# Query tiles moved by one block, narrow products paired across heads, and the largest tile's heads in two PSUM tiles

## The chip, the cores and the metric

The kernel runs on one core of a Trainium2 chip. Five engines work side by side, each through its own instructions in program order: PE (matrix products and transposes), DVE (vector work, reductions, copies), ACT (exponentials and copies), POOL (vector work, and it issues some DMAs) and SP (it issues DMAs). They wait for each other by semaphores. The metric is the device time of one execution in microseconds (us), the median of several runs.

## What is computed

Two stages. First attention over 8 batches and 8 heads, 576 positions of 64 features, float32; a position sees its own block of 64 and all blocks before it. Then a mixture of experts over the 4608 positions: a gate chooses one of 8 experts for each position, every expert keeps the 80 positions with the largest gate weights, and two products (512 to 1024 to 512) are made for these.

```python
def _attn_ref(q, k, v):
    scores = scale * np.matmul(q, k.transpose(0, 1, 3, 2))
    mask = (pos // 64)[:, None] >= (pos // 64)[None, :]
    scores = np.where(mask, scores, -1000000000.0)
    scores = scores - np.max(scores, axis=-1, keepdims=True)
    attn = np.exp(scores)
    attn = attn / (np.sum(attn, axis=-1, keepdims=True) + 1e-09)
    return np.matmul(attn, v)

def _moe_ref(x, w_gate, w1, w2, capacity):
    logits = x @ w_gate
    expert_idx = np.argmax(logits, axis=1)
    ...
    for e in range(E):
        ...                     # the 80 largest gate weights of expert e
        h = np.maximum(x[tok_idx] @ w1[e], 0.0)
        out[tok_idx] = gate_w[tok_idx, None] * (h @ w2[e])
```

## The kernel before

**Pairs and turns.** The unit of attention is a pair of heads (`Pair`); there are 32. The 64 features of head 0 lie on partitions 0 to 63, those of head 1 on 64 to 127, so products of both heads run side by side in two halves of PE. The main loop (`for i in range(-3, n + 2)`) makes one turn per pair. A turn carries out the table `TURN`, an order written out by hand: each entry has an offset, a step and arguments, and acts on pair `i` + offset. So a turn mixes steps of up to six pairs. The instructions of an engine are in the order in which the table's steps issue them.

**Tiles.** The 9 blocks of queries are cut into tiles. Tile u (0 to 3) holds blocks 2u and 2u+1, 128 queries, and sees keys 0 to 128(u+1); its first block may not see the last 64 of them, and a product of `mrow` and `mneg` (L481) adds a large negative number there. Tile "4" holds block 8 of both heads, 64 queries each on 128 partitions, and sees all 576 keys (L490).

**PSUM.** The scores use a ring of two tiles of two banks, `sc`: first the largest tile ("3", both heads, 512 columns each), then tiles 2 and 0 together ("20"), tile 1 ("1") and tile 4 ("4"). All else on PE (transposes, values, gate) uses a ring of four tiles of one bank, `pm`.

**Steps of a pair.** `load` issues q and k (SP, L426), `load_v` issues v (POOL, L434 and L436). `prep` transposes q (0, with a scaling on POOL, L459) and k (1) on DVE (L456). `scores` makes the products (L474) and the mask (L481). `max` reduces each row on DVE (L495, L499 for tile 4). `soft` takes the exponential on ACT, with the sums of the rows (L503; L508 for tile 4). `back` transposes the exponentials on PE (L539; L522 for a piece named 44): A is tile 3, B tiles 1 and 2, C the rest; 16 narrow transposes each into two `pm` tiles. `take` copies a `pm` tile to SBUF, on ACT (L579) or DVE (L581) by the table `TAKE`. `values` multiplies with v (L569): 0 for positions 0 to 511 and 1 for the last 64. `flip` turns the result on DVE (L290) and stores it.

**The gate of a batch.** When the four pairs of a batch are done, nine steps (reciprocals, store, logits of two halves, and so on to the table of weights) are put on a list, `todo`; the three entries `step` of a turn take one each. The gate's work thus lies in three of a batch's four turns.

**Behind attention** the candidates are selected (line 700 on), gate weights are picked with one-hot products on PE (L822) from columns that POOL builds (L748), and the experts' products run (L894, L907).

## Time and profile before

| | us |
|---|---|
| median of 3 runs | 433.95 |
| lowest, highest | 432.39, 435.62 |
| profiled execution, its own time | 433.55 |
| its span in the trace | 431.8 |

| engine | busy, us | share of the span |
|---|---|---|
| PE | 407.2 | 94% |
| DVE | 281.9 | 65% |
| ACT | 272.7 | 63% |
| POOL | 137.4 | 32% |

Shares over the whole span mix two stages: attention takes the first three quarters, the experts the rest, where DVE and ACT are nearly idle. A view of a stretch says more than the page's averages, and the timeline of one turn more than both. PE overlaps the end of a matrix product with the beginning of the next, so in its timeline the starts are to be read, not the ends.

### The profile page before, as it was taken

What the parts mean: (1) busy time and instruction counts of PE and PEld (TensorE: products, weight loads), DVE (VectorE), ACT (ScalarE), POOL (GpSimd) and SP (SyncE); (2) the same over time, 40 slices, a digit from 0 to 9 for tenths busy, and PEclk for the clock granted to TensorE, in tenths of its full rate; (3) what the DMA queues carried; (4) which work ended last, traced back from release to release, by engine and by line L of the source; (5) the groups of instructions that cost most, each with busy time, mean ns of one, the idle gap of its engine ahead of it and who ended that gap; (6) DMA issues with size and microseconds to landing.
All of it is one profiled execution on the core that took longest, in us unless ns stands there. A gap on an engine that the chain in (4) does not pass through costs nothing. (4 is left out here: it accounts for less than half of the span.)

```text
span 431.8 us, 15597 instructions
## 1 busy us (share of the span) xinstructions
PE 407.2 (94%) x6454; PEld 287.8 (67%) x6454; DVE 281.9 (65%) x566; ACT 272.7 (63%) x868; POOL 137.4 (32%) x236
## 2 busy tenths in 40 slices
PE   7899999999999999999999999999886799999982
PEld 3566666666666666666666666666654699999981
DVE  5778888888797888879778887986584122111111
ACT  2988888798888879888887988889531110111000
POOL 9523343233344323334432333540037300000011
PEclk9999999999999999999999999999998699999998
DMA  9999958995997899499688969899986999999821
GB/s 149 156 130 180 176 93 199 147 181 120 210 177 105 204 137 188 118 206 179 106 199 134 177 137 208 181 372 330 275 176 187 325 304 310 286 320 328 310 81 37
DMA packets 201276, 84.59 MB, mean 196 GB/s; under 512 B 167677, under 2 KB 183805, under 8 KB 201200
## 3 DMA queue, kind: packets, MB, share of 16 engines
q1 hardware_dynamic: 190112, 53.37, 63.4%
q0 software_dynamic: 9888, 29.87, 22.2%
q8 instruction: 53, 0.87, 0.9%
q10 hardware_dynamic: 1200, 0.30, 0.3%
q14 instruction: 23, 0.19, 0.2%
HBM read 63.38 MB, written 20.33 MB: 194 GB/s over the span
## 5 line engine op out<-in xcount | busy, mean ns | idle before, releaser
L503 ACT ACTIVATE P<-sc,negm 128x128 f32<-128x128 f32 (+3 forms) x256 | 133.3, 531 | 9.9 <-DVE negm L495 8.3
L495 DVE TENSOR_REDUCE negm<-sc 128x2 f32<-128x1024 f32 (+3 forms) x128 | 100.5, 811 | 38.7 <-PE sc L481 38.7
L474 PE MATMUL sc<-T,T 64*128 64x128 f32 (+3 forms) x512 | 92.8, 460 | 1.9 <-DVE T L452 1.2
L539 PEld LDWEIGHTS pm<-ident,P 64*128 64x128 f32 x1536 | 55.7, 139 | 32.6 <-ACT xT L579 11.0
L459 POOL TENSOR_SCALAR T<-T 128x576 f32<-128x576 f32 x31 | 20.5, 661 | 171.9 <-DVE T L456 162.6
L539 PE MATMUL pm<-ident,P 64*128 64x64 f32 x1536 | 67.7, 227 | 2.0 <-ACT P L508 0.4
L569 PE MATMUL pm<-PT,vn 128*64 128x128 f32 (+1 forms) x512 | 60.7, 379 | 0.0
L474 PEld LDWEIGHTS sc<-T,T 64*128 64x128 f32 x512 | 41.7, 187 | 22.2 <-issue 7.1
L503 ACT ACTIVATION_READ_ACCUMULATOR P<-sc,negm 128x1 f32 x256 | 52.8, 206 | 0.0
L434 POOL DMA_DIRECT2D vn<-in_v_dram x64 | 50.1, 785 | 1.4 <-issue 1.4
L569 PE MATMUL pm<-PF,vn 128*64 128x64 f32 (+1 forms) x768 | 48.2, 247 | 0.9 <-ACT PF L579 0.9
L569 PEld LDWEIGHTS pm<-PT,vn 128*64 128x64 f32 x512 | 33.5, 137 | 22.9 <-issue 22.9
L456 DVE STREAM_TRANSPOSE T<-ld 128x576 f32<-128x576 f32 x62 | 47.4, 764 | 0.0
L894 PE MATMUL ps<-xsT,w 128*64 128x80 f32 x1024 | 42.4, 241 | 5.1 <-issue 5.0
L579 ACT COPY PF<-pm 128x512 f32<-128x512 f32 x64 | 34.4, 589 | 15.7 <-PE pm L539 15.7
L894 PEld LDWEIGHTS ps<-xsT,w 128*64 128x64 f32 x1024 | 39.1, 142 | 7.6 <-issue 6.9
L581 DVE COPY PT<-pm 128x512 f32<-128x512 f32 x64 | 43.5, 680 | 0.3 <-ACT xT L579 0.3
L490 PE MATMUL sc<-T,T 64*64 64x288 f32 x256 | 38.0, 415 | 0.6 <-ACT P L503 0.6
L919 ACT ACTIVATE hT<-ps 128x320 f32<-128x320 f32 x16 | 7.0, 437 | 49.3 <-PE ps L894 49.3
L579 ACT COPY PT<-pm 128x512 f32<-128x512 f32 x64 | 37.8, 591 | 0.0
L508 ACT ACTIVATE P<-sc,negm 128x576 f32<-128x576 f32 x32 | 23.7, 741 | 21.3 <-DVE negm L499 21.3
L569 PEld LDWEIGHTS pm<-PF,vn 128*64 128x64 f32 x768 | 32.0, 137 | 7.4 <-ACT PF L579 1.1
(185 smaller groups left out, 468.0 us busy)
## 6 DMA issues: line engine op xcount, KB each, us to landing
w<-in_moe_w_dram SPq DMA_DIRECT2D x48, 512.0 KB, 5.0
out_dram<-zero POOLq DMA_DIRECT2D x18, 512.0 KB, 4.2
ld<-in_q_dram SPq DMA_DIRECT2D x124, 72.0 KB, 3.9
ld<-in_k_dram SPq DMA_DIRECT2D x124, 72.0 KB, 3.9
vn<-in_v_dram POOLq DMA_DIRECT2D x64, 128.0 KB, 4.3
w<-in_moe_w_dram POOLq DMA_DIRECT2D x4, 2048.0 KB, 14.3
xs<-Y SPq DMA_DIRECT2D x28, 288.0 KB, 4.9
xs<-Y SPq DMA_DIRECT2D x16, 72.0 KB, 10.1
```

The source lines that it names most:

```text
L434: nc.gpsimd.dma_start(self.vn[:, h], v[b, h0 + h, 0:512].rearrange("(j p) d -> p j d", p=P))
L456: nc.vector.transpose(t, self.nat[x].rearrange("p g d -> p (g d)"))
L474: nc.tensor.matmul(s[:, h, c:c + P * (u + 1)], lhsT=self.T[0][r, P * u:P * (u + 1)], rhs=self.T[1][r, 0:P * (u + 1)], start=(x == 0), stop ...
L490: nc.tensor.matmul(s[r, c, 0:288], lhsT=self.T[0][r, 512:S], rhs=self.T[1][r, 288 * c:288 * (c + 1)], start=True, stop=True)
L495: nc.vector.tensor_reduce(self.negm[:, u], self.s[g][:, :, c:c + P * (u + 1)], axis=AX.X, op=ALU.max, negate=True)
L503: nc.scalar.activation(Pt[self.i % 2][u][:, h], self.s[g][:, h, c:c + P * (u + 1)], AF.Exp, bias=self.negm[:, u, h:h + 1], scale=1.0, accu ...
L508: nc.scalar.activation(Pt[self.i % 2][4][:, 0:S].rearrange("p (c k) -> p c k", c=2), self.s["4"][:, :, 0:288], AF.Exp, bias=self.negm[:, 4 ...
L539: nc.tensor.transpose(pt[c][:, n_ * BLK:(n_ + 1) * BLK], from_[r, P * j:P * (j + 1)], ident[r, r])
L569: nc.tensor.matmul(to, lhsT=lhs, rhs=rhs, start=(n_ == 0), stop=(n_ == len(steps) - 1))
L579: nc.scalar.copy(*self.out.pop((what, x)))
L581: nc.vector.tensor_copy(*self.out.pop((what, x)))
L894: yield nc.tensor.matmul(dst(b)[64 * c:64 * (c + 1)], lhsT=w_[:, a, col:col + 64], rhs=x_[:, a], start=(a == 0 and b == 0), stop=(a == n - ...
```

## The change

**Tiles.** The query tiles are moved by one block. Block 0 of both heads is now tile "4", with 64 keys; tile u holds blocks 2u+1 and 2u+2 and sees 128(u+1) + 64 keys. Its scores are made in two products, the whole part and a tail of 64 keys; the mask hides the tail from the tile's first block. Head 1's tail is put ahead of its whole part, head 0's behind, so that the tails of both heads are neighbours in SBUF and one transpose turns both.

**Products of a head with its equal.** Tile 4's scores are two products over 128 partitions with `qz`, copies of the first query block in which the other head's half is zero (`alone`, made on POOL). In the same way the turned tails are multiplied with `vz`, the odd blocks of v with the other head's half zero, eight products 64 wide in `values` 0. `values` 1 keeps two of its ten products. `load_v` loads the odd blocks for each head into `vz`, two DMAs of 64 KB, in place of one of 32 KB.

**PSUM.** The two heads of the largest tile take one `sc` tile each. Tile 4's scores move to a `pm` tile, `L`, one turn ahead; the same tile then holds the piece 44 and `values` 1 of the pair before. Tiles 1 and 0 now share an `sc` tile ("10"), and tile 2 has one.

**Order.** `TURN` is written anew: back B moves to the next turn, prep is made two pairs ahead, loads five pairs ahead, flip three turns behind. The gate has twelve steps, which the table places itself, at offsets -2 to -5. Three entries of `TAKE` change (A1 to ACT, C0 and `values` 1 to DVE).

**Behind attention** the numbers of positions are put right: a fourth column is picked with the gate weights (L822's product is 32 wide instead of 24).

```diff
-TAKE = {"back": {"A0": "a", "A1": "v", "B0": "a", "B1": "v", "C0": "a", "C1": "a", "44": "a"},
-        "values": {0: "a", 1: "a"}}
+TAKE = {"back": {"A0": "a", "A1": "a", "B0": "a", "B1": "v", "C0": "v", "C1": "a", "44": "a"}, "values": {0: "a", 1: "v"}}
...
 TURN = (
...
-    (1, "prep", 1),
...
+    (2, "prep", 1),
+    (5, "load"),
 )
...
         def load_v(self):
...
-            self.vt = VT[self.i % 4]
-            nc.gpsimd.dma_start(self.vt[0:BLK], v[b, h0:h0 + 2, 512:576].rearrange("h p d -> p h d"))
+            self.vz = VZ[self.i % NVZ]
+            for h in range(2):
+                half = v[b, h0 + h, BLK:S].rearrange("(u c k) d -> k u c d", c=2, k=BLK)[:, :, 1]
+                nc.gpsimd.dma_start(self.vz[h * BLK:(h + 1) * BLK, h], half)
...
+        def alone(self):
+
+            self.qz = QZ[self.i % 2]
+            for h in range(2):
+                r = slice(h * D, h * D + D)
+                nc.gpsimd.tensor_copy(self.qz[r, h], self.T[0][r, 0:BLK])
...
         def scores(self, g):
...
+            place = [ps_s.tile([P, 2, 512], F32, name="sc") for _ in range(2 if g == "3" else 1)]
...
+            for u in us:
+                w = P * (u + 1)
+                pair(u, 0, w, [at(u, h)[0] for h in range(2)], u > 0, u == 3)
+                pair(u, w, w + BLK, [at(u, h)[1] for h in range(2)], u == 3)
...
         def scores_4(self):
...
+            self.L = L = ps_m.tile([P, 512], F32, name="pm")
+            for h in range(2):
+                nc.tensor.matmul(L[h * D:(h + 1) * D, P + BLK:P + 2 * BLK], lhsT=self.qz[:, h], rhs=self.T[1][:, 0:BLK],
+                                 start=True, stop=True)
...
         def back(self, x):
...
+                self.PF = big.tile([P, 12, BLK], F32, name="PF")
+                blocks = [b for h in range(2) for b in ((0, h, 0), (2, h, 2))]
...
+            if x == "C":
+                for u in (3, 1, 2, 0):
+                    r = slice(BLK, P)
+                    flat = row[u].rearrange("p h w -> p (h w)")
+                    nc.tensor.transpose(pt[1][:, (4 + u) * BLK:(5 + u) * BLK], flat[r, P * (u + 1):P * (u + 2)], ident[r, r])
...
         def values(self, half):
...
-                     (2, 8, 9, 3 * P, 512), (2, "X", 5, 2 * P, 3 * P)]
+                     (2, 8, 9, 3 * P, 512), (2, "X", 1, 2 * P, 3 * P)] + \
+                    [(u, "H", 8 + u, P * u + BLK, P * (u + 1)) for u in range(NT - 1)]
...
-        for i in range(-3, n + 2):
+        for i in range(-5, n + 6):
```

Three places show how the order moves. The rows of an engine stand as the program issues them; the names are output, then inputs, `x` counts equal instructions.

PE before, the second half of a turn: scores of tile 1 and their mask, back A, `values` 1 of the pair before (PF is the turned tile 4, `vt` the last block of v), tile 4's scores and the beginning of back B.

```order
L474 MATMUL sc<-T_2027,T_1935 128x256 x2
L481 LDWEIGHTS mrow
L481 MATMUL sc<-mneg,mrow 128x64
L481 LDWEIGHTS mrow
L481 MATMUL sc<-mneg,mrow 128x64
L539 MATMUL pm<-ident,P_0_131 128x64 x16
L569 MATMUL pm<-PF,vn 64x64 x8
L569 MATMUL pm<-pl_135,vt_139 64x64 x2
L490 MATMUL sc<-T_2027,T_1935 64x288 x4
L539 MATMUL pm<-ident,P_0_128 128x64 x2
```

PE after, the end of a turn and the first products of the next: `values` 0 with eight products on `vz`, `values` 1 of the same turn's pair, back A, and then at once the largest tile's scores, each in two widths.

```order
L700 MATMUL pm<-PF,vz_137 64x64 x8
L680 MATMUL pm<-pl_133,vn 64x64 x2
L654 MATMUL pm<-ident,P_0_130 128x64 x16
L571 MATMUL sc<-T_2205,T_2167 128x512 x2
L571 MATMUL sc<-T_2205,T_2167 128x64 x2
```

Tile 4's 288-wide products and most of `values` 1 are gone from this place, back B stands in the next turn, behind back C, and eight products on `vz` are added.

DVE before, one turn in the middle of attention: the transposes of k and q, three reductions of tiles 3, 2 and 0 and one of tile 1 (each for both heads), the copies of A1 and B1, the flip, and tile 4's reduction.

```order
L456 STREAM_TRANSPOSE T_3246<-ld_2923 128x576
L495 TENSOR_REDUCE negm<-sc 128x2 x3
L456 STREAM_TRANSPOSE T_3338<-ld_2924 128x576
L495 TENSOR_REDUCE negm<-sc 128x2
L581 COPY PT<-pm 128x8x64
L290 STREAM_TRANSPOSE Y<-xT 128x18x32
L499 TENSOR_REDUCE negm<-sc 128x1
L581 COPY PT<-pm 128x2x2x128
```

DVE after, one turn: reductions with `128x1` are of one head (3,1, then 3,0, later 2,1 and 2,0), those with `128x2` of both (tiles 0 and 1); L620 is tile 4 of the next pair.

```order
L617 TENSOR_REDUCE negm<-sc 128x1
L716 COPY PF<-pm 128x256
L617 TENSOR_REDUCE negm<-sc 128x1
L311 STREAM_TRANSPOSE Y<-xT 128x18x32
L716 COPY PT<-pm 128x2x2x128
L617 TENSOR_REDUCE negm<-sc 128x2
L617 TENSOR_REDUCE negm<-sc 128x1
L620 TENSOR_REDUCE negm<-pm 128x1
L617 TENSOR_REDUCE negm<-sc 128x2
L617 TENSOR_REDUCE negm<-sc 128x1
```

The largest tile's reduction is in two halves with the copy of C0 between them, the transposes of q and k stand at the end of the turn, and no reduction of tile 4 with 576 elements is left.

DVE at the program's start, before: the last copies that build the first pair's T, the transpose of q of the second pair, three reductions of the first pair, and only then the transpose of k of the second pair.

```order
L453 TENSOR_SCALAR T_228<-sc 128x64
L456 STREAM_TRANSPOSE T_268<-ld_201 128x576
L495 TENSOR_REDUCE negm<-sc 128x2 x3
L456 STREAM_TRANSPOSE T_323<-ld_202 128x576
L495 TENSOR_REDUCE negm<-sc 128x2
```

The same place after.

```order
L539 TENSOR_SCALAR T_227<-sc 128x64
L620 TENSOR_REDUCE negm<-pm 128x1
L544 STREAM_TRANSPOSE T_277<-ld_207 128x576
L544 STREAM_TRANSPOSE T_282<-ld_208 128x576
L617 TENSOR_REDUCE negm<-sc 128x1 x2
```

Both transposes of the second pair have moved ahead of the first pair's large reductions.

## Rows read from the trace of the kernel before

**Rows 1.** Windows: stretch, us; busy PE, PEld, DVE, ACT, POOL; PE clock, DMA share, GB/s.
```profile
15.83:306.41 290.58, 288.93 (x4053) 186.88 (x4050) 238.76 (x410) 247.64 (x795) 100.79 (x154) 1.00 0.90 179
...
271.00:306.00 35.00, 34.86 (x502) 22.58 (x498) 27.59 (x50) 30.53 (x100) 11.57 (x17) 1.00 0.98 310
```
**Rows 2.** Timeline of PE over a turn and into the next: start, us, line.
```profile
173.77 1.08 PE L474 MATMUL sc<-T,T 64*128 64x512 f32 x4
174.68 0.20 PE L481 MATMUL sc<-mneg,mrow 64*128 64x64 bf16 x2
175.02 0.71 PE L539 MATMUL pm<-ident,P 64*128 64x64 f32 x16
175.56 1.09 PE L474 MATMUL sc<-T,T 64*128 64x384 f32 x8
...
176.64 0.30 PE L522 MATMUL pm<-ident,P 128*64 128x128 f32 x1
176.89 0.44 PE L569 MATMUL pm<-PF,vn 128*64 128x128 f32 x4
...
179.20 0.70 PE L474 MATMUL sc<-T,T 64*128 64x256 f32 x4
...
180.39 0.69 PE L569 MATMUL pm<-PF,vn 128*64 128x64 f32 x16
...
181.12 1.19 PE L490 MATMUL sc<-T,T 64*64 64x288 f32 x8
182.24 0.71 PE L539 MATMUL pm<-ident,P 64*128 64x64 f32 x16
...
184.62 0.20 PE L481 MATMUL sc<-mneg,mrow 64*128 64x64 bf16 x2
184.65 0.69 PE L539 MATMUL pm<-ident,P 64*128 64x64 f32 x16
```
**Rows 3.** Timeline of ACT in the same turn; in brackets the wait and its releaser.
```profile
174.13 0.74 ACT L508 ACTIVATE P<-sc,negm 128x576 f32<-128x576 f32 x1 [0.77 <-DVE negm L499]
...
178.49 0.57 ACT L503 ACTIVATE P<-sc,negm 128x384 f32<-128x384 f32 x1
...
180.76 0.47 ACT L503 ACTIVATE P<-sc,negm 128x256 f32<-128x256 f32 x1
...
183.15 0.74 ACT L508 ACTIVATE P<-sc,negm 128x576 f32<-128x576 f32 x1 [0.78 <-DVE negm L499]
```
**Rows 4.** Groups of DVE instructions by shape: busy us, mean ns, idle before, releaser.
```profile
L581 DVE COPY PT<-pm 128x512 f32<-128x512 f32 x64 | 43.5, 680 | 0.3 <-ACT xT L579 0.3
...
L499 DVE TENSOR_REDUCE negm<-sc 128x1 f32<-128x576 f32 x32 | 24.2, 758 | 13.1 <-PE sc L490 12.8
L495 DVE TENSOR_REDUCE negm<-sc 128x2 f32<-128x512 f32 x32 | 21.9, 683 | 28.9 <-PE sc L481 28.9
```
**Rows 5.** Timeline of the program's start, 5 to 16 us.
```profile
5.36 1.93 SPq L426 DMA_DIRECT2D ld<-in_k_dram  x4
...
9.21 2.42 DVE L495 TENSOR_REDUCE negm<-sc 128x2 f32<-128x1024 f32 x3 [0.44 <-PE sc L481]
...
11.55 0.77 DVE L456 STREAM_TRANSPOSE T<-ld 128x576 f32<-128x576 f32 x1
...
15.47 1.08 PE L474 MATMUL sc<-T,T 64*128 64x512 f32 x4
```
**Rows 6.** Timeline of PE and ACT at the end of attention.
```profile
296.86 1.13 PE L474 MATMUL sc<-T,T 64*128 64x512 f32 x4
...
311.80 0.59 ACT L579 COPY xT<-pm 128x512 f32<-128x512 f32 x1 [2.21 <-PE pm L569]
```
**Rows 7.** DMA queues (packets, MB, share), then one issue: count, KB, median us.
```profile
q1 hardware_dynamic: 190112, 53.37, 63.4%
q0 software_dynamic: 9888, 29.87, 22.2%
...
ld<-in_k_dram SPq DMA_DIRECT2D x124, 72.0 KB, 3.9
```

More of the change, by code (lines that the diff above doesn't have):

```diff
@@ new lines @@
+    (-1, "take", "back", "B1"),
+    (-4, "gate", "gexp"),
+    (0, "soft", 3, 0),
+    (1, "begin"),
+    (1, "scores_4"),
+    (0, "back", "44"),
+    (0, "scores", "10"),
+    (-1, "take", "back", "C1"),
+    (0, "scores", "2"),
+    (-1, "take", "back", "B0"),
+    (-3, "gate", "lt"),
+    (0, "max", 0),
+    (0, "soft", 0, 1),
+    (0, "max", 2, 1),
+    (-5, "gate", "gturn"),
+    (1, "max_4"),
+    (0, "soft", 0, 0),
+    (-5, "gate", "turn2"),
+    (0, "soft", 2, 1),
+    (0, "max", 1),
@@ L55 @@
+    (-2, "gate", "logits0"),
+    (-2, "gate", "logits1"),
+    (-1, "values", 0),
+    (0, "take", "back", "44"),
+    (0, "max", 2, 0),
+    (-2, "gate", "recip"),
+    (-3, "gate", "lm"),
+    (-2, "gate", "lgc0"),
+    (0, "soft", 1, 0),
+    (0, "values", 1),
+    (-2, "gate", "lgc1"),
+    (-5, "gate", "wcopy"),
+    (0, "soft", 1, 1),
+    (2, "prep", 0),
+    (0, "soft", 2, 0),
+    (-4, "gate", "gb"),
     (0, "back", "A"),
-    (1, "prep", 1),
-    (-1, "take", "back", "44"),
-    (0, "soft", 2, 0),
@@ L327, in logits2, with scaled @@
                                                   self.lgT[:, tok0(t):tok0(t) + n], ident)
+        def scaled(self, half, ends=(4, NT)):
+            la = self.la[half]
+            rs = self.rs
+            t0, t1 = (0, *ends)[half:half + 2]
+            if half == 0:
+                self.lg = sm.tile([P, NT, E], F32, name="lg", bufs=2)
             for u0, u1, n in ((t0, min(t1, NT - 1), P), (NT - 1, t1, BLK)):
@@ L382, in turn2, with wcopy, part, done @@
                         tile_position=(0, 32 * g))
+        def wcopy(self):
+            tp = self.tp
             nc.vector.tensor_copy(Wt[:, :, :, self.b, :].rearrange("p h t a -> p t a h"),
                                   tp[:, 0:8 * NT].rearrange("p (t a h) -> p t a h", t=NT, h=2))
+        def part(self, name):
+            if name in ("logits0", "logits1"):
+                self.logits_(int(name[-1]))
+            elif name in ("lgc0", "lgc1"):
+                self.lgc(int(name[-1]))
+            elif name == "lt":
+                for half in range(2):
+                    self.turned_(half)
+            elif name == "lm":
+                for half in range(2):
+                    self.scaled(half)
+            elif name == "gturn":
+                self.turn(nc.gpsimd)
+            elif name == "turn2":
+                self.turn2_()
+            else:
+                getattr(self, name)()
+            if name == "recip":
+                self.done()
+        def done(self):
+            self.over += 1
+            if self.over == 2:
+                self.store()
     Wt = sel.tile([P, 2, NT, 8, 4], F32, name="Wt")
@@ L518, in back @@
             if x == "44":
-                dst = PL[self.i % 2][0:BLK]
-                self.last = ps_m.tile([P, 512], F32, name="pm")
+                self.last = pairs[self.i + 1].L if self.i + 1 < n else ps_m.tile([P, 512], F32, name="pm")
                 src = self.last[0:BLK, 0:P]
-                nc.tensor.transpose(src, row[4][:, 512:S], ident)
-                self.out["back", x] = (dst, src)
+                nc.tensor.transpose(src, row[4], ident)
+                self.out["back", x] = (PL[self.i % 2][0:BLK], src)
                 return
@@ L557, in values @@
             if half == 1:
-                steps = [(j, None, j, 0, BLK) for j in range(5)]
+                av = self.last[:, P:P + BLK]
+                for h in range(2):
+                    nc.tensor.matmul(av[h * D:(h + 1) * D], lhsT=self.vn[:, h, 0], rhs=PL[self.i % 2][:, h * BLK:(h + 1) * BLK],
+                                     start=True, stop=True)
+                self.out["values", 1] = (self.bt.xT[:, self.pr, 512:S], av)
+                return
+            av = ps_m.tile([P, 512], F32, name="pm")
@@ L628, in tile_attn_moe @@
             for d, what, *args in TURN:
-                if what == "step":
-                    step()
-                elif 0 <= i + d < n and not (what == "flip" and i + d >= n - NP):
-                    getattr(pairs[i + d], what)(*args)
-                if i == 0 and what == "scores" and args == ["20"]:
+                j = i + d
+                if not 0 <= j < n:
+                    continue
+                if what == "gate":
+                    if j % NP == NP - 1 and j < n - 1:
+                        batches[j // NP].part(args[0])
+                    continue
+                if what == "flip" and j >= n - NP:
+                    continue
+                getattr(pairs[j], what)(*args)
+                if what == "flip" and j % NP == NP - 1:
+                    batches[j // NP].done()
+                if j == 0 and what == "scores" and args == [LAST]:
                     warm(WARM0, ps_m.tile([P, 512], F32, name="pm"))
+                if what == "take" and args[0] == "values" and j >= n - NP and pairs[j].values_taken():
+                    pairs[j].flip()
+                    pairs[j].bt.store_pair(pairs[j].pr)
             if i == n:
```

240 lines of the change are left out of this document (130 added, 110 removed).

## The prediction

> **What bounds the kernel now.** I read first the busy times by stretch. From the first exponential of a small tile to the last, 15.83 to 306.41 us, PE is busy for 288.93 of 290.58 us, ACT for 247.64, DVE for 238.76, and the DMA share is .90 [rows 1]. This is the stretch that the change rewrites. The small tile's steps run 32 times, once per pair of heads (its reduction's row says so [rows 4]), so 31 turns fill the 290.58 us and a mean turn is 9.37 us. Then PE's timeline of one turn [rows 2]. A turn without gate work lasts 9.02 us, read on ACT from one small-tile exponential at 174.13 to the next at 183.15 [rows 3]; 31 of those are 279.6, so the gates of seven batches show (290.58 - 279.6) / 7 = 1.57 us each.
>
> PE is not idle-free in a plain turn: between the mask at 174.68 and transposes C at 175.02 it waits for the small tile's exponential, about .31 us (in a turn with gate work C follows the mask at once, 184.62 and 184.65) [rows 2, 3]. So a plain turn is 8.71 us of PE work and .31 of waiting. DVE and ACT are far from idle as well (about 7.7 and 8.0 us per mean turn [rows 1]); DVE waits long for scores, 28.9 us before one form of the reduction and 13.1 before the small tile's [rows 4].
>
> **What leaves PE and what comes.** Removed: the small tile's eight 288-wide products, 181.12 to 182.24, 1.12 us; and of the second values step, 180.39 to 181.12, .73 us for 20 instructions, all but the products of one pair of heads [rows 2]. Those 20 give a price: two concurrent 64-wide passes about .07 us, so a float32 product (two passes) of both heads about .13 to .14. Added at that price: the 64-key tails of four tiles, 4 x .13; eight 64-wide products in the first values step, four pairs, .53; the new small tile, .14; the rest of the second values step, .14. Transposes C lose eight narrow ones and gain four single ones, which I cost at nothing: four pairs against four singles, the same four steps. Net 1.85 - 1.33 = .52 less: **8.19 us of PE work**.
>
> **What the new order makes of it.** The largest tile now takes both score tiles in PSUM, so no other scores are ahead of it. I walk a turn from its first score product at 0, with durations of before. The result of the largest tile is there at 1.24: .91 to the mask and .20 for it, as at 173.77 to 174.88 [rows 2], and .13 of tail. DVE reduces head 1 (576 elements, .76 [rows 4]) to 2.04, with .04 of handoff; the exponential of 576 on ACT is seen by PE .89 after its start, as at 174.13 and 175.02 [rows 2, 3], so at 2.96. In this time PE has C, B, the next small tile and 44. B waits .2 for a PSUM tile that the small tile's exponential frees, and 44 is done at about 2.75, so PE **waits .4 in all**. From 2.96: scores of tiles 1, 0 and 2 and back A (before 1.08 for two tiles, 175.56 to 176.64, and 1.19 for the third and A, 179.20 to 180.39 [rows 2]; two tails more, .27); first values 2.31 (176.89 to 179.20) and .53; second .14. That ends at 8.48.
>
> The second path is the ring through DVE and ACT. Head 0 of the largest tile is reduced behind head 1 and a copy of 256 columns (half of .68 [rows 4], .35): 3.15; its exponential frees the tile for tile 2's scores at 4.07; these take 1.07: 5.14; then the reduction of 448 and that of tile 1's 640 (.758 and .683 for 576 and 512 [rows 4] are 1.17 ns an element: .61 and .83): 6.62; two exponentials of 320 at .50 each (between .47 and .57, those of 256 and 384 [rows 3]): 7.65; the last of 448, .65 and .15 until PE sees it: 8.45. Then the next largest tile may be written. Both paths end within .1 us, and neither has a slack of importance. DVE's records overlap by up to .08, which I give back for handoffs that were not counted. **I take 8.5 us**.
>
> DVE has four small additions and ACT about as many columns as before; their sums, some 7.9 us a turn, lie below 8.5 and cost nothing more unless they come late (first rival). On the gate: 1.57 per batch is kept although it is cut into twelve steps, and two turns of a batch lose the .31 that the gate used to fill: 2.2. POOL's zero-padded copies of the first query block lie on an engine that is busy for 100.79 of 290.58 us [rows 1], and are made one turn earlier than they are used; if that cover were gone they would cost two short copies, some .3 us a turn. In the selection POOL builds a fourth column and PE's product of the columns is 32 wide instead of 24; it is a few short instructions beside the experts' products, which keep PE busy there: 0, at most 1.
>
> So from the second pair's first score product to the last pair's: 30 x 8.5 + 7 x 2.2 = 270.4. Before it was 15.47 [rows 5] to 296.86 [rows 6], 281.4. **Gain 11.0**.
>
> **What the start costs.** Before, DVE reduces the first pair's scores at 9.21, and transposes k of the second pair at 11.55 only after that [rows 5]. Now both transposes of the second pair stand ahead of the first large reduction on DVE. k of that pair is issued from 5.36 to 7.3 [rows 5] and a load takes a median of 3.9 us to land [rows 7]: 11.2, and .77 of transpose: the first reduction starts at about 11.9. From that point in a turn (1.28) to the next turn's start (8.5) it is 7.2: 19.1 instead of 15.47, **3.6 lost**. Were k there at once, 1.9 would be lost; as PE is idle there longer, its clock could fall too, which I estimate at up to 1 more. At the end, from the last pair's first score product to the last wide copy of an attention result, it was 296.86 to 311.80, 14.9 [rows 6]; now 8.5 and, of the next turn, C, B, the C1 copy and the values, about 6: 14.5, **.4 gained**.
>
> Sum: 433.55 - 11.0 + 3.6 - .4 = 425.75, against the profiled execution's own 433.55 (span 431.8 and 1.75 around it); the median of the runs, 433.95, is .4 higher. I say 425.8.
>
> **What DMA has to carry.** v's odd blocks are loaded for both heads into zero-padded tiles: 128 KB instead of 32, 96 KB more per pair, 3.1 MB in all. By the software queue, which took 22.2% of 431.8 us for 29.87 MB, a MB costs 3.2 us; by the other, 63.4% for 53.37 MB, mostly small pieces, 5.1 [rows 7]. That is .32 to .52 us per turn on 8.4 (.90 of 9.37): 8.75 to 8.95 against a mean turn of 9.0 (8.5 and 2.2 / 4). Full, but a stretch of 35 us had .98 [rows 1], with turns as long as others; I cost it at nothing, and loads are now issued five pairs ahead.
>
> The Trainium skill ("DMA: Bandwidth & Descriptors", Specifications) speaks against this part: a transfer needs at least 512 bytes for line rate, and v's pieces here are 256. The dearer price of the second queue is what agrees with it; by that price the sum stays, and the third rival gets its chance.
>
> **The rivals.**
> *The ring is slower (slower than before).* The path above has eight handoffs between PE, DVE and ACT, and DVE already waits 28.9 us for one form of scores [rows 4]. If each handoff takes .06 us more than I gave it, or the gate's steps are in the way by as much, a turn is 8.98: 30 x .48 = 14.4 more, 440. It decides for slower by 1% from .42 us per turn on. Against it: the handoffs counted here fit rows of before.
> *PE remains the bound.* If the waits vanish into one another, a turn is 8.19: 416.5. Against it: PE has nothing to do at 2.75.
> *The change is eaten by DMA (no change).* 261.5 us of DMA time in the stretch grow by up to 16 to 277.6; at a share of .98 they need 283, at .95 292: with the start, 430 to 438, about 434.
>
> **How the numbers follow.** Forecast .56, with its own range 420 to 431 (turn 8.3 to 8.65); slow ring .15; PE .08; DMA .14; two smaller losses together (a start later by 3 and the seven gates dearer by 5) .07, about 434. About 1% is what a measurement of this kernel can tell from no change: below 429.6 and above 438.3. Faster: .52 of the forecast and PE's .08, .60. Slower: .10 of the ring and .04 of DMA and the small losses, .14. Same: the rest, .26. The range, 415 to 438, leaves out the slower end of the ring and of DMA, and a small part of PE's case.
>
> **What would show it.** Right: first score products of the largest tile 8.4 to 8.6 us apart in plain turns; PE waiting about .4 before the scores of tiles 1 and 0, for head 1's exponential; the second pair's first at 18 to 20; the small tile's products near .14. Wrong: waits above .6 in a turn at tile 2's scores or before the largest tile (slow ring); k or v tiles named as what DVE or PE waited for (DMA); eight narrow value products well above .53, or DVE busy above 8.3 per turn.

## The result: about one per cent slower, and the profile after

The changed kernel takes 439.11 us (median of 18 runs, 436.38 to 441.87), the kernel before beside it 434.99 (18 runs): 1.0095 of it, interval 1.0069 to 1.012. The forecast was 425.8 with a range to 438; the time lies above the range, and the sign is wrong.

The span of the profiled execution went from 431.8 to 436.5 us, 4.7 more. Three sections, cut at score products that both traces have, hold all of it:

| section | before | after | difference | forecast |
|---|---|---|---|---|
| start to second pair's first score product | 15.47 | 20.82 | +5.35 | +3.6 |
| from there to the last pair's | 281.39 | 278.86 | -2.5 | -11.0 |
| from there to the end | 134.96 | 136.77 | +1.8 | -.4 |

The last row is good to some 3 us only: a second trace of the changed kernel (below) has 20.88 and 278.8 in the first two rows, but 139.5 in the last. So the turns did get shorter, by a quarter of what I had worked out, and the two ends together cost more than the turns gave. The page of after, with the clock that was granted to PE in 40 slices:

```profile
PEclk9599999999999999999999999999998799999996
...
q1 hardware_dynamic: 190112, 53.37, 65.9%
q0 software_dynamic: 10912, 33.02, 25.9%
```

The second digit, the slice from 10.9 to 21.8 us, is a 5: PE had half its clock there. The windows of after say the same (stretch and length, then busy PE, PEld, DVE, ACT, POOL, then PE clock, DMA share, GB/s), beside the one of attention, which answers to [rows 1]:

```profile
20.80:299.70 278.90, 272.19 (x4181) 207.35 (x4177) 237.68 (x494) 246.07 (x742) 138.05 (x246) 1.00 0.98 177
...
10.00:15.00 5.00, 4.33 (x23) 2.71 (x23) 2.45 (x4) 1.69 (x6) 4.78 (x10) 0.50 1.26 165
15.00:20.00 5.00, 5.00 (x30) 3.41 (x28) 2.50 (x5) 2.20 (x8) 0.71 (x2) 0.50 1.35 160
```

PE is now idle for 6.7 us of attention (1.7 before), and the DMA share has risen from .90 to .98.

**One plain turn.** The timeline of after, all engines, over the same kind of turn as [rows 2, 3]; from 150.96 to 159.68 it is 8.72 us:

```profile
150.96 1.25 PE L571 MATMUL sc<-T,T 64*128 64x512 f32 x8
...
152.04 0.19 PE L578 MATMUL sc<-mneg,mrow 64*128 64x64 bf16 x2
...
152.28 0.76 DVE L617 TENSOR_REDUCE negm<-sc 128x1 f32<-128x576 f32 x1 [0.33 <-PE sc L578]
...
153.15 0.74 ACT L623 ACTIVATE P<-sc,negm 128x576 f32<-128x576 f32 x1 [0.60 <-DVE negm L617]
...
153.51 0.34 PE L609 MATMUL pm<-T,qz 128*64 128x64 f32 x4 [0.20 <-DVE PF L716]
...
154.04 1.18 PEld L571 LDWEIGHTS sc<-T,T 64*128 64x128 f32 x16 [0.15 <-ACT P L623]
154.04 1.32 PE L571 MATMUL sc<-T,T 64*128 64x256 f32 x16
...
155.25 1.03 PE L571 MATMUL sc<-T,T 64*128 64x384 f32 x8
...
156.24 0.44 PE L700 MATMUL pm<-PF,vn 128*64 128x128 f32 x4
...
158.46 0.63 PE L700 MATMUL pm<-PF,vz 128*64 128x64 f32 x16
...
158.92 0.29 PE L680 MATMUL pm<-pl,vn 128*64 128x64 f32 x4
158.94 0.63 ACT L623 ACTIVATE P<-sc,negm 128x448 f32<-128x448 f32 x1
...
159.14 0.71 PE L654 MATMUL pm<-ident,P 64*128 64x64 f32 x16
...
159.68 0.73 PE L571 MATMUL sc<-T,T 64*128 64x512 f32 x2
```

The reader sees the shape that the prediction described: the largest tile's scores, their reduction and exponential, PE waiting a little, and from 154.04 on unbroken PE work. The waits are .20 at the new small tile (L609) and .15 before the second scores, where PEld, PE's weight load, waits for head 1's exponential; .4 in all was forecast. 154.04 is .89 after the exponential's start at 153.15, as in [rows 2, 3]. Only the lengths are others: 3.08 until the second scores start (forecast 2.96) and 5.64 of work behind them (5.52).

### The profile page after: what moved, and what is told of

Read it like the earlier page. It is cut to its first block, busy times and chain, and to the rows that moved or that the text cites. A ratio compares the mean times of both kernels' runs of the same rounds, so it can differ in the third digit from the quotient of the medians.

```text
span 436.5 us, 16417 instructions
## 1 busy us (share of the span) xinstructions
PE 402.9 (92%) x6710; PEld 318.5 (73%) x6710; DVE 286.3 (66%) x663; ACT 278.9 (64%) x836; POOL 177.1 (41%) x340
## 3 DMA queue, kind: packets, MB, share of 16 engines
q1 hardware_dynamic: 190112, 53.37, 65.9%
q0 software_dynamic: 10912, 33.02, 25.9%
## 4 chain that ended last, share of the span: by engine, by line
PE 77%; DVE 9%; issue 5%; POOL 3%; DMA 2%; ACT 2%; SPq 0%; POOLq 0%; DVEq 0%; ACTq 0%
PE sc L571 22%; PE pm L700 18%; PE ps L1032 10%; PE av L1032 7%; PE pm L654 6%; DVE negm L617 5%; PE pm L609 2%; PE pm L340 2%; DVE PF L716 2%; PE pm L638 1%; DMA ld<-in_q_dram 1%; PE pm L357 1%; ACT P L623 1%; PE pm L1075 1%; PE pm L1045 1%
## 5 line engine op out<-in xcount | busy, mean ns | idle before, releaser
L623 ACT ACTIVATE P<-sc,negm 128x576 f32<-128x576 f32 (+3 forms) x256 | 147.6, 581 | 35.4 <-DVE negm L617 30.1
L617 DVE TENSOR_REDUCE negm<-sc 128x1 f32<-128x576 f32 (+2 forms) x192 | 129.1, 687 | 36.6 <-PE sc L578 36.5
L571 PE MATMUL sc<-T,T 64*128 64x64 f32 (+4 forms) x1024 | 116.0, 361 | 1.0 <-ACT P L623 0.6
L571 PEld LDWEIGHTS sc<-T,T 64*128 64x128 f32 x1024 | 84.5, 191 | 30.6 <-issue 14.5
L714 ACT COPY PT<-pm 128x512 f32<-128x512 f32 x96 | 53.9, 599 | 2.7 <-PE pm L654 0.6
L522 POOL DMA_DIRECT2D vz<-in_v_dram x64 | 40.8, 657 | 0.9 <-DMA vn<-in_v_dram 0.7
L1032 PE MATMUL av<-hT,w 128*64 128x80 f32 x896 | 33.3, 234 | 1.4 <-issue 1.3
L1032 PEld LDWEIGHTS av<-hT,w 128*64 128x64 f32 x896 | 31.8, 137 | 3.0 <-issue 3.0
L311 DVE STREAM_TRANSPOSE Y<-xT 128x576 f32<-128x576 f32 x32 | 24.6, 767 | 4.3 <-ACT xT L714 4.3
L700 PE MATMUL pm<-PF,vn 128*64 128x128 f32 x256 | 26.5, 285 | 0.0
```

What stands on the lines that cost most here:

```text
L311: nc.vector.transpose(self.Y[:, :, pr], self.xT[:, pr])
L522: nc.gpsimd.dma_start(self.vz[h * BLK:(h + 1) * BLK, h], half)
L571: nc.tensor.matmul(to[h], lhsT=self.T[0][r, BLK + P * u:BLK + P * (u + 1)], rhs=self.T[1][r, k0:k1], start=start, stop=stop)
L617: nc.vector.tensor_reduce(to, src, axis=AX.X, op=ALU.max, negate=True)
L623: nc.scalar.activation(Pt[self.i % 2][u][:, h], self.s[u][h], AF.Exp, bias=self.negm[:, u, h:h + 1], scale=1.0, accum_out=self.bt.sums[:, ...
L700: nc.tensor.matmul(to, lhsT=lhs, rhs=rhs, start=(n_ == 0), stop=(n_ == len(steps) - 1))
```

## Experiments

Each run stands against the kernel before on its own chip. The kernel before itself takes a median of 430.8 to 435.0 us from chip to chip. The changed kernel, unaltered, ran again only beside the three runs that follow it below; the others are read mainly from their traces. Times of whole runs are medians; a score product's time is its start in the trace.

### The padded tiles zeroed on DVE

```diff
     for t_ in VZ:
         for h in range(2):
-            nc.gpsimd.memset(t_[h * BLK:(h + 1) * BLK, 1 - h], 0.0)
+            nc.vector.memset(t_[h * BLK:(h + 1) * BLK, 1 - h], 0.0)
```

(and the same for QZ.)

> The changed kernel with the zeroing of the padded tiles (vz, qz) on DVE instead of POOL; nothing else. In the changed kernel DVE waits 1.99 us for an index pattern that POOL makes only at 7.86 us (before: at 5.95), behind those memsets; the first score product starts at 9.70 (before 8.02), PE idles in pieces and the granted clock is .50 from 10 to 20 us; the second pair's first product starts at 20.8. Theory A (memsets on POOL, then the clock): first product at about 8.0, granted clock 1.0 through the first turn, second pair's first product at 16 to 17.5, the whole 3.5 to 5 us shorter, 434 to 436. Theory B (the step of my forecast: the second pair's transposes ahead of the first reduction, waiting for k): first product earlier, but the second pair's still at 18.5 or later and at most 2 us gained. In both the turns behind it stay as they are (8.72 us plain).

437.59 us, 1.017 (1.0089 to 1.0252) of the kernel before. The first score product starts at 10.49, later than in the changed kernel, and the clock is .50 again. A miss of the experiment: DVE has to make the identity matrix first, and zeroing stood ahead of it. It decides nothing but where the zeroing must not be.

### v's blocks copied instead of loaded

```diff
-                half = v[b, h0 + h, BLK:S].rearrange("(u c k) d -> k u c d", c=2, k=BLK)[:, :, 1]
-                nc.gpsimd.dma_start(self.vz[h * BLK:(h + 1) * BLK, h], half)
+                nc.gpsimd.dma_start(self.vz[h * BLK:(h + 1) * BLK, h, NT - 2], v[b, h0 + h, 512:S])
...
+                nc.gpsimd.tensor_copy(self.vz[h * BLK:(h + 1) * BLK, h, 0:NT - 2], self.vn[0:BLK, h, 1:NT - 1])
```

> The changed kernel, but three of the four padded blocks of v are copied on POOL from the v tile that is loaded anyway, and only the last block is loaded for each head: 32 KB per pair instead of 128, as before the change. Theory A (DMA saturation costs only where stores and weight loads are waited for, at the end of attention): DMA share in attention falls from .98 to about .90, plain turns stay at 8.72 within .03, and 1 to 3 us are gained behind the last pair, where the gather now starts 3.2 us after its indices are ready: 436 to 438. Theory B (DMA bounds the turns): plain turns fall to 8.5 and the whole by 8 or more, 431 or less. Theory C (DMA plays no part): within 1 us of the changed kernel.

437.41 us, 1.0146 (1.0056 to 1.0237). Its window of attention:

```profile
38.90:290.00 251.10, 243.79 (x3747) 184.95 (x3745) 215.25 (x453) 220.53 (x667) 136.22 (x275) 1.00 0.87 163
```

The share fell to .87 (.97 in the same window of the changed kernel) and the plain turns are 8.72 as before. So DMA does not set the turn: theory B falls. The end gained next to nothing (136.6 us from the last pair's scores to the end, 136.8 and 139.5 in the changed kernel's two traces), so theory A's second half is not shown by this run alone. Some turns with gate work became longer, 9.53 instead of 9.08, where POOL's copies stood ahead of the gate's.

### Without the eight narrow value products

```diff
-                     (2, 8, 9, 3 * P, 512), (2, "X", 1, 2 * P, 3 * P)] + \
-                    [(u, "H", 8 + u, P * u + BLK, P * (u + 1)) for u in range(NT - 1)]
+                     (2, 8, 9, 3 * P, 512), (2, "X", 1, 2 * P, 3 * P)]
```

> The changed kernel without the eight narrow products of the turned tails with the padded v (.46 us of PE in each turn); this part of the attention result is left out, the loads and transposes stay. Theory A (a turn is the time until head 1's exponential of the largest tile, 3.08, and then PE's unbroken work, 5.64): plain turns of 8.72 - .46 = 8.26, 30 turns, 13.8 us less: about 425. Theory B (the ring through the two score tiles, DVE and ACT, is the bound or close behind, at my 8.45): plain turns of 8.45 or more, at most 8 us less, with PE waiting before the largest tile's products.

428.7 us, .9971 (.9932 to 1.0011) of the kernel before. The plain turn of a batch is 8.31 instead of 8.72, and the one ahead of it 8.95 instead of 9.42: .41 and .47 less, what was taken from PE. But the turn of 9.08 stays at 9.07, and the three plain turns behind the start stay at 8.78. In both kinds the trace shows PE waiting in the middle of the largest tile's scores; here in a turn of 9.19 (9.21 in the changed kernel) behind a plain one, and by the same .24 in the turn at 38.55, one of the three:

```profile
155.86 0.63 ACT L623 ACTIVATE P<-sc,negm 128x448 f32<-128x448 f32 x1
...
156.15 1.61 PE L571 MATMUL sc<-T,T 64*128 64x512 f32 x6
...
156.63 0.62 PEld L571 LDWEIGHTS sc<-T,T 64*128 64x128 f32 x4 [0.24 <-ACT P L623]
```

Head 1's score tile is free only when the last exponential of the pair before, started at 155.86, has been read out. So both theories hold, each in its turns: PE's own way sets the changed kernel's plain turn, and the ring through the score tiles stands right behind it. A batch gave back 1.11 us of the 1.84 that PE was relieved of.

### The first weight loads a turn earlier

```diff
-            if n - 3 <= i < n - 3 + FW0:
+            if n - 4 <= i < n - 4 + FW0:
```

> The changed kernel with the four first expert weight loads (2 MB each, POOL's queue) one turn earlier. They are issued at 281.6, 290.7 and 296.2 us (two), 3.6 us before the last pair's first score product; before the change it was 6.2 us. Theory A (they delay the last stores and so the gather): last stores land earlier, the gather follows its indices by about .5 instead of 3.2 us, the first gathered rows are there 4 to 6 us after it instead of 8.4, and 2 to 4 us are gained, 435 to 437. Theory B (the stores are late by SP's own queue): gather unchanged, within 1 us of the changed kernel.

440.35 us, 1.022 (1.0116 to 1.0324). Timelines of DVE and POOL:

```profile
295.32 1.32 POOL L522 DMA_DIRECT2D vz<-in_v_dram  x2 [1.78 <-DMA w<-in_moe_w_dram]
...
297.10 0.78 DVE L544 STREAM_TRANSPOSE T<-ld 128x576 f32<-128x576 f32 x1 [5.70 <-DMA ld<-in_k_dram]
...
337.91 0.97 POOL L923 DMA_INDIRECT xg<-xs,gi  x1 [0.51 <-DVE gi L930]
...
340.86 0.89 DVE L1020 TENSOR_TENSOR xn<-xg 80x128 f32<-80x128 f32 x4 [3.23 <-DMA xg<-xs,gi]
```

Both theories were too simple. The gather is prompt, as theory A said: first rows 3.23 us after its indices, where the changed kernel waits 9.95. From the last pair's scores to the end it is 131.2 us, 5.6 less. But the last turn became 17.83 us: DVE waited 5.70 for k while the 2 MB loads were under way, PE stood still for 6.12, and its granted clock was .50 from 297.7 to 304.5.

### The changed kernel again

> The changed kernel itself, unaltered, beside the others on the same chip. Every theory: 1.0 to 1.2% over the kernel before; first score product at 9.7 us, second pair's at 20.8, last pair's at 299.7, gather about 3 us behind its indices.

438.94 us, 1.0089 (1.0053 to 1.0125): the verdict repeats. First score product at 9.71, second pair's at 20.88, last pair's at 299.71. From there to the end it is 139.5 us, 2.7 more than in the first trace.

### The padded v tiles zeroed in the first turn

```diff
-    for t_ in VZ:
-        for h in range(2):
-            nc.gpsimd.memset(t_[h * BLK:(h + 1) * BLK, 1 - h], 0.0)
...
                 if j == 0 and what == "scores" and args == [LAST]:
+                    for t_ in VZ:
+                        for h in range(2):
+                            nc.gpsimd.memset(t_[h * BLK:(h + 1) * BLK, 1 - h], 0.0)
                     warm(WARM0, ps_m.tile([P, 512], F32, name="pm"))
```

> The changed kernel with the zeroing of the padded v tiles moved on POOL from the program's start into the first turn (DVE, where the run before put it, had to make the identity matrix first and was as late). Theory A (POOL's memsets delay the index pattern that DVE waits for): first score product at 8.0 to 8.4 instead of 9.70. Clock: if the half speed from 10 to 20 us came from PE's longer pauses before 9.7, it stays at 1.0 and the second pair's first product is at 15.5 to 17; if it came from the pauses of the first turn itself, it is still .5 there and that product is at 19 to 19.5. Theory B (transposes of the second pair ahead of the first reduction, my forecast's step): it is at 18 to 19 with the clock at 1.0.

437.91 us, 1.0066 (1.0035 to 1.0097), 1.0 us under the changed kernel beside it, with intervals that overlap. The start in its timeline, and two windows:

```profile
8.33 1.30 PE L571 MATMUL sc<-T,T 64*128 64x512 f32 x8 [0.43 <-DVE negm L620]
...
10.05 0.78 DVE L544 STREAM_TRANSPOSE T<-ld 128x576 f32<-128x576 f32 x1 [1.05 <-DMA ld<-in_k_dram]
...
10.75 1.38 DVE L617 TENSOR_REDUCE negm<-sc 128x1 f32<-128x576 f32 x2
...
11.57 0.77 PE L609 MATMUL pm<-T,qz 128*64 128x64 f32 x4 [1.92 <-POOL qz L555]
```

```profile
10.00:15.00 5.00, 3.43 (x25) 2.91 (x25) 2.09 (x3) 1.55 (x4) 4.70 (x11) 0.63 1.33 165
15.00:20.00 5.00, 4.87 (x39) 3.29 (x36) 3.63 (x8) 3.33 (x13) 1.63 (x6) 0.69 1.38 154
```

The first scores came 1.4 us earlier, so POOL's zeroing had delayed them. Now my forecast's step appears too: the reduction waits behind the transpose, and that for k, until 10.75. And the clock fell all the same, at 11.27, late in a pause of 1.92 us in which PE waited for POOL's copies of the second pair's first query block (`qz`). So a pause of the first turn itself was enough: the second pair starts at 19.63.

### Products that fill PE's pause

```diff
+                if j == 0 and what == "scores" and args == ["3"]:
+                    warm(WARM3, ps_m.tile([P, 512], F32, name="pm"))
```

(on top of the edit before, WARM3 = 4.)

> As the run on the start, and PE has four 512-wide products of the identity more right behind the first pair's largest scores, where it waits for the first exponential. If PE's pauses in the first turn cost the clock: granted clock 1.0 there, and the second pair's first score product at 15.5 to 17 instead of 19 or later. If not: no difference, or up to .5 us later by the products themselves.

435.92 us, 1.0042 (1.001 to 1.0075), 3.0 under the changed kernel. The clock is 1.00 from 15 us on, with .76 in the five before:

```profile
10.00:15.00 5.00, 5.00 (x39) 3.50 (x37) 2.58 (x4) 1.56 (x4) 4.74 (x11) 0.76 1.37 161
15.00:20.00 5.00, 4.34 (x48) 2.92 (x45) 3.58 (x8) 4.79 (x17) 3.28 (x10) 1.00 1.33 153
```

The second pair starts at 18.12, later than the 15.5 to 17 expected if the pauses were all: a dip from 9.0 to 12.4 us is left, and the first turn's own order.

### Both edits on DMA together

```diff
+    (0, "vcopy"),
     (0, "soft", 2, 1),
...
-            if n - 3 <= i < n - 3 + FW0:
+            if n - 4 <= i < n - 4 + FW0:
```

(with the copies of the second experiment, at a later place of the turn.)

> The copy of v's blocks on POOL (placed behind the gate's work of a turn this time) and the first weight loads one turn earlier, together. Alone, the earlier weights made the gather prompt (.45 us behind its indices, first rows 3 us later) but stalled the last turn by 8.4 us, in which DVE waited for k and POOL for v behind the weights. Theory A (DMA saturation is what made that stall): with 96 KB per pair less to carry the last turn stays under 12 us, the gather is prompt, and the whole is 3 to 5 us under the changed kernel. Theory B (the 2 MB loads block v's and k's loads whatever the share): the last turn is again 14 us or more, and nothing is gained.

438.5 us, 1.0078 (1.0047 to 1.0108): .4 under the changed kernel beside it, within the noise of the two, so the 3 to 5 us expected of the whole are not shown. The trace supports theory A in its places: the last turn is 9.51, the gather starts .45 behind its indices, and the last section takes 134.5 us (136.8).

```profile
328.96 0.97 POOL L927 DMA_INDIRECT xg<-xs,gi  x1 [0.51 <-DVE gi L934]
...
333.02 1.57 DVE L1024 TENSOR_TENSOR xn<-xg 80x128 f32<-80x128 f32 x6 [4.34 <-DMA xg<-xs,gi]
```

### Less on DVE in the ring

```diff
-    (1, "max_4"),
...
     (0, "max", 2, 0),
+    (1, "max_4"),
...
-TAKE = {"back": {... "C0": "v", ...
+TAKE = {"back": {... "C0": "a", ...
```

> The changed kernel with less on DVE between the largest tile and the last exponential: the small tile's reduction (.21 us) stands behind the other tiles' instead of ahead of tile 1's, and the copy C0 (.41) is made on ACT, which is idle there. The ring through the score tiles gets some .3 us shorter; PE's own way (3.08 until the exponential of head 1 is seen, then 5.64 of work) stays. Theory A (the two ways tie: PE's 8.72, ring 8.78): the three turns of 8.78 behind the start fall to 8.72, plain turns stay at 8.72, the gate's turn of 9.08, in which DVE has most to do, falls by .1 to .3; the whole 1 to 2 us less, 437 to 438. Theory B (the ring sets the plain turn too): all of them fall by .2 or more, 6 us or more less.

437.76 us, 1.0171 (1.0116 to 1.0225). The plain turn stayed at 8.72, as theory A had it, but none fell: the turns of 8.78 stayed too, and the gate's became 9.17 (9.08 before this edit). A turn of 8.78 in its timeline:

```profile
38.70 1.31 PE L571 MATMUL sc<-T,T 64*128 64x512 f32 x8
...
40.95 0.74 ACT L623 ACTIVATE P<-sc,negm 128x576 f32<-128x576 f32 x1 [0.27 <-DVE negm L617]
...
43.90 0.42 ACT L623 ACTIVATE P<-sc,negm 128x192 f32<-128x192 f32 x1 [0.43 <-DVE negm L617]
...
46.72 0.63 ACT L623 ACTIVATE P<-sc,negm 128x448 f32<-128x448 f32 x1
...
47.48 1.31 PE L571 MATMUL sc<-T,T 64*128 64x512 f32 x8
```

From the largest tile's first exponential to the last of the turn it is 5.77 us, as in the changed kernel (153.15 to 158.94, 5.79), although .6 us of DVE work was taken out of that stretch. From 43.90 on ACT goes from one exponential to the next, with one copy of .25 between, without a pause. So, by this timeline, the ring does not go by tile 2's scores and tile 1's reduction, as I had drawn it, but by the second scores, tile 0's reduction and ACT's row of exponentials; DVE's other work has slack there.

### All that helped, together

The padded v tiles zeroed in the first turn, WARM3, v's copies, the weights a turn earlier and the ring's two edits, as above, and these two: k of the second pair transposed behind the two reductions of the first pair's largest tile, and a conversion of the capacity (for the gate) on DVE instead of POOL.

```diff
+                if j == 1 and what == "prep" and args == [1]:
+                    continue
                 getattr(pairs[j], what)(*args)
+                if j == 0 and what == "max" and args == [3, 0]:
+                    pairs[1].prep(1)
...
-        nc.gpsimd.tensor_copy(cf, ci)
+        nc.vector.tensor_copy(cf, ci)
```

> All that helped, together: padded v tiles zeroed in the first turn, four products that keep PE's clock behind the first largest scores, the second pair's k transposed behind the first pair's reductions instead of ahead of them, v's blocks copied on POOL, the first weight loads a turn earlier, the small tile's reduction later, C0 on ACT, and the capacity's conversion on DVE. Theory (the parts add up): second pair's first score product at 17 instead of 20.8, last one about 4.5 us earlier than the changed kernel's, gather .5 us behind its indices: about 7 us under the changed kernel, 432, .5 to 1% under the kernel before. Rival (the loads that were made early stall the last turns, as in the run with the early weights alone): the last turn 14 us or more, no better than the changed kernel.

430.61 us, .9987 (.9962 to 1.0013) of the kernel before, on the chip where the ring run took 437.76. The gather is .45 behind its indices, the last turn 9.52, the last section 131.8 us. Against the ring run's trace the start is 1.7 us shorter, the middle .4 and the last section 5.3: most of the gain lies at the end. The last pair came only 2.2 us earlier than in the changed kernel, not 4.5, and the second pair's start at 19.25 missed its 17. The clock was lower (.77 from 10 to 15 us), but that is not all, for the run with WARM3 alone had .76 there and 18.12. Two of the edits lengthened the first turn: PE waits .59 us at the second pair's small tile for the transpose of k that was moved back, where the run with WARM3 waits for nothing, and 1.17 at the second values step for the small tile's reduction (.52 there, for a copy). The next run adds three products that compute nothing behind the first turn's early preparation:

```diff
+                if j == 0 and what == "prep" and args == [1]:
+                    warm(3, ps_m.tile([P, 512], F32, name="pm"), w=idle)
```

> The run before with three products of zeros more on PE, behind the transposes of the first pair, where PE pauses for .6 us ahead of its first scores. If the clock still dips around 9 to 12 us because of that pause: granted clock 1.0 there and .5 to 1 us less. If not: the same within .3 us in the second pair's start.

430.26 us, .9979 (.9951 to 1.0007). Now the clock holds, the first turn falls from 10.52 to 9.49, and the second pair starts at 18.00:

```profile
5.00:10.00 5.00, 4.61 (x30) 2.83 (x29) 2.10 (x8) 1.35 (x4) 4.00 (x10) 1.00 1.07 143
10.00:15.00 5.00, 3.85 (x38) 2.77 (x38) 2.59 (x5) 1.93 (x6) 4.70 (x11) 1.00 1.33 165
15.00:20.00 5.00, 3.84 (x53) 3.15 (x55) 4.01 (x8) 4.68 (x18) 3.94 (x11) 1.00 1.35 146
```

Last, this kernel with the ring's two edits taken back:

```diff
+    (1, "max_4"),
...
     (0, "max", 2, 0),
-    (1, "max_4"),
...
-TAKE = {"back": {... "C0": "a", ...
+TAKE = {"back": {... "C0": "v", ...
```

> The last run's kernel with the small tile's reduction and the copy C0 where the change put them: those two edits left the plain turns at 8.72 and made the gate's turn of 9.08 one of 9.17. Theory A (the turn's two ways run over PE and over ACT, DVE is on neither): that turn is 9.08 again, the plain ones 8.72, seven batches less .6 us in all, everything else as in the last run: .3 to .6% under the kernel before. Theory B (DVE is on the way and its relief helped): plain or gate turns .1 or more longer, 1 to 3 us more than the last run.

429.75 us, .9987 (.996 to 1.0014). The gate's turn is 9.08 again and the plain ones 8.72, which is theory A; the forecast gain over the kernel before is not shown. With all that was found the new order is as fast as the old one, and no version here beats it by more than the measurement can tell.

## Why the prediction was wrong, point by point

**The plain turn** was to be 8.5 and is 8.72; 30 turns make 6.6 us of the 12.5 by which the sections miss; single turns make 2.1, the start 1.8 and the end 2.2, each below. The mechanism was right: time until head 1's exponential is seen, then unbroken PE work, and the run without the narrow products took from these turns what it took from PE. The term that failed is "scores of tiles 1, 0 and 2 and back A", which I put at 2.54 and which takes 2.74 (154.04 to 156.24, and .54 for A). Three tiles have three tails; I counted two, though the sum of PE's work ahead of it had all four tiles' tails. And a tail is .17, not .13 to .14: the largest tile's mask starts 1.08 after its first product, .17 more than the .91 of [rows 2]. I had priced it by 64-wide value products that use all 128 rows; the nearest rows, the scores' own, were not consulted. Why a tail takes .17 no run shows. The other pieces nearly cancel: the eight narrow products .46 instead of .53, the rest of the first values 2.22 instead of 2.31, the second values .22 instead of .14. The first part is .12 late, in handoffs: the reduction starts 152.28 - 150.96 = 1.32 behind the first product (1.28), the exponential at 2.19 (2.07). The .08 of overlap that I gave back for handoffs that were not counted was too little on a path with PE, DVE and ACT in turn.

**The second path** was forecast at 8.45 and measured near 8.78, where the run without the narrow products laid it bare. It tied with PE's way, as said, but I had drawn it through the wrong stations, tile 2's scores and tile 1's reduction: the DVE relief left the turns of 8.72 and 8.78 as they were. In the timeline it goes by ACT's unbroken exponentials; no run took work from these to prove it.

**The gate** was right: a batch's four turns are 9.42, 8.72, 9.08 and 9.83, together 2.17 over four plain ones, forecast 2.2.

**Single turns** that no term held make 2.1 us in all: the first (9.32), one of 10.53 in which DVE waits 1.08 for POOL's conversion of the capacity, one of 9.46 and one of 10.11, and smaller ones. The conversion on DVE turned 10.53 into 9.88.

**The start** lost 5.35 instead of 3.6, and not for my reason. Timeline of after:

```profile
7.86 0.14 POOL L234 IOTA iota_c<- 128x16 f32 x1
...
8.04 0.18 DVE L236 TENSOR_TENSOR iota_c<-sameR,iota_c 128x16 f32<-128x16 f32 x1 [1.99 <-POOL iota_c L234]
...
9.60 1.43 DVE L544 STREAM_TRANSPOSE T<-ld 128x576 f32<-128x576 f32 x2
9.70 2.28 PE L571 MATMUL sc<-T,T 64*128 64x512 f32 x8 [0.43 <-DVE negm L620]
...
12.07 1.42 DVE L617 TENSOR_REDUCE negm<-sc 128x1 f32<-128x576 f32 x2 [1.04 <-PE sc L578]
...
20.82 1.26 PE L571 MATMUL sc<-T,T 64*128 64x512 f32 x5
```

The first reduction starts at 12.07, and I had said 11.9, so that the agreement is luck: both transposes are done by then and it waits for PE. The first scores are 1.7 us late (8.02 before), and 1.4 of that is the zeroing of the v tiles on POOL, which I had given no term: with it moved they start at 8.33. At half clock they take 2.28 instead of 1.25. The forecast's step lay hidden under this; it came up when the zeroing was moved, and smaller than I had it: k is there at 10.05, not 11.2, and the reduction starts at 10.75. The cover that I took for granted for POOL's copies of the first query block is missing at the start: PE waits .67 us for them in the changed kernel and 1.92 with the zeroing moved.

The clock was named and bounded "up to 1 more". It costs as much or more: four products that fill a pause took the first turn from 11.30 to 9.49 us, and three further ones, from .77 to 1.00 in the clock of 10 to 15 us, took it from 10.52 to 9.49. These are single traces; three of an unedited start have 11.0 to 11.2.

**The end** lost 1.8 instead of gaining .4. Up to the gather's indices .4 was gained as forecast (326.39 - 296.86 = 29.5 before, 328.81 - 299.68 = 29.1 now). Behind them, first before, then after:

```profile
326.39 0.17 DVE L796 TENSOR_REDUCE gi<-ps 80x8 int32<-80x16 f32 x1 [0.93 <-PE ps L778]
329.90 0.89 DVE L882 TENSOR_TENSOR xn<-xg 80x128 f32<-80x128 f32 x4 [3.34 <-DMA xg<-xs,gi]
```

```profile
296.19 1.76 POOL L260 DMA_DIRECT2D w<-in_moe_w_dram  x2
...
326.56 0.71 SPq L323 DMA_DIRECT2D xs<-rs  x1
...
328.81 0.17 DVE L930 TENSOR_REDUCE gi<-ps 80x8 int32<-80x16 f32 x1 [0.93 <-PE ps L912]
...
330.55 1.13 POOL L923 DMA_INDIRECT xg<-xs,none  x1 [3.11 <-issue]
331.99 0.98 POOL L923 DMA_INDIRECT xg<-xs,gi  x1 [0.30 <-issue]
...
338.92 2.27 DVE L1020 TENSOR_TENSOR xn<-xg 80x128 f32<-80x128 f32 x8 [9.95 <-DMA xg<-xs,gi]
```

The last weight loads left POOL 3.5 us ahead of the last pair's scores, 6.2 before the change; SP's last store goes out at 326.56 (317.57 before), the gather's first instruction waits 3.11 us for the stores, until 330.55, the first read by indices goes out at 331.99, and the rows come 9.95 us after the indices instead of 3.34. In this trace 4.4 of these 6.6 us are made up later, 3.1 of them in pauses of PE among the experts' products; that their weights had landed by then is a guess. The second trace of the same kernel makes up nothing: its rows come 7.83 us after the indices, and from there to the end it is 102.4 us, 101.9 before. The clock has a part here too, which no run separates: from 330 to 345 us it was .66 before and after, .58 in the second trace, and 1.00 in the run with all that helped. The weights a turn earlier gave a prompt gather; that alone moved the wait to k and v; with fewer bytes for v, both were gone.

**DMA** was given a rival, about 434, in which the turns grow. The turns do not (the run at a share of .87 has the same 8.72), but the price was real: the software queue took 25.9% of 436.5 us against 22.2% of 431.8 [rows 7], 17.2 us more for 3.15 MB more, 5.5 us per MB, a little over the dearer of the two prices. The Trainium skill ("DMA: Bandwidth & Descriptors", Specifications) has pieces under 512 bytes below line rate, and this trace agrees: 5.5 us per MB for 256-byte pieces, 3.2 for that queue's mix. But the other queue's packets, the same 53.37 MB, took 13.9 us more as well (65.9% against 63.4% [rows 7]), so time that the queues cost each other is in these prices, and the whole came to 31 us where I had 16 at most. What the share costs is paid where something waits for the last transfer, at the end.

**The rival that would have ended slower**, a ring dearer by .06 at each handoff, gave 440, near the time measured; that is no merit of it. The turns are 8.72 and not 8.98, and more than half of the distance to 8.5 is a miscounted tail.

What stays open: how much of the first turn's remaining 2.0 us over the kernel before (9.49 against 7.45) is the order with both score tiles taken, which was not varied; how the 7 us between the ring run and the run with all that helped divide among its edits; and the whole-run gain of the two DMA edits alone, which the medians do not show.

## What to carry to other kernels

Price a new instruction by the row nearest to it in operation and shape, not by its width alone, and count pieces from the order after, one by one; here .2 us in a turn that repeats thirty times was half the error. When a steady loop is rewritten, give its two ends terms of their own: setup work that is put on an engine at the start can delay the first product, PE can lose its clock in the pauses that follow, and transfers at the end delay what is fetched last. Where two paths tie, relieving one shows nothing; take work off the supposed bound first, and see which wait comes up.

## What the runs showed of the hardware

- PE's granted clock at the start. In the changed kernel it fell to .50, which is 1.2 of 2.4 GHz, at 9.86 us, behind pauses of 1.53 and .43 us, and rose at 20.10. With the zeroing moved and four products that compute nothing it fell at 8.98, behind pauses of .64 and .43, and rose at 12.39; with seven it was 1.00 from 5 to 20 us, in spite of later pauses of 1.15 and 1.16. The kernel before, with pauses of 1.19, .68 and .57, kept 1.00. So the longest pause alone does not tell whether the clock falls.
- In the largest tile's scores two 64-wide float32 products, one of each head, over 64 rows took .17 together; eight in a series over 128 rows (four pairs) took .46, .115 a pair.
- With a 2 MB load put ahead of them on the software queue, v's 256-byte pieces and k were both late, though k comes by the other queue: v's issue waited 1.78 us and DVE 5.70 us for k, and the turn took 17.83. With 96 KB less of v to carry per pair the same loads, as early, left that turn at 9.51.
